# Moving the opening's arithmetic off GpSimd in a GFNet mixing + MLP kernel: filter products added in PSUM, places for all weight pieces early, the filter loaded by two queues

## Chip, cores and metric

The kernel runs on one core of one Trainium2 chip. The metric is the device time of one execution in microseconds (us). Engines are named as in the profile: PE is TensorE, DVE is VectorE, ACT is ScalarE, POOL is GpSimd and SP is SyncE. L12 is line 12 of the kernel that the view belongs to. The changed kernel has other line numbers than the kernel before: the products L312 to L315 become L311 to L314, the weight multiplications L596 and L602 become L597 and L603, the first main loop matmul L405 becomes L408, and L590 (the step that joins a weight's sign and exponent) keeps its number. The sum of a weight's two parts moves from GpSimd at L584 to DVE at L592.

## The reference

```python
X = np.fft.rfft(x, axis=1)                  # x: (8, 3008, 256) fp32
Y = X * (filt_r + 1j * filt_i)[None]        # filter: (1505, 256), complex
y = np.fft.irfft(Y, n=3008, axis=1)
h = y.reshape(24064, 256) @ w_in            # (256, 2048), float64 in memory
g = np.where(h > 0, h, np.exp(np.minimum(h, 0)) - 1)
out = g @ w_out                             # (2048, 256), float64 in memory
```

## The kernel before

The transforms are matmuls (3008 = 47 x 64), and the two matrix products of the MLP use seven products in place of eight. The main loop works on one batch of the MLP while it transforms the next. Before the loop stands an **opening**: batch 0 is transformed alone, and beside it the float64 weights, 16 pieces of 512 KB, are turned into fp32. Each piece goes through a split (two DVE masks), four ACT instructions, a sum of two parts f + l, and a join (one DVE instruction that adds the sign, then multiplications into `w_in` or `w_out`; after every second piece four additions that make the Strassen sets). A split with its conversion and the join of the piece before is called a tick here.

Batch 0's transform is worked in eight groups g. `b_unit` does eight matmuls into PSUM, then four DVE products with the filter, and adds them; `bi_unit` transforms back and evacuates by ACT; `y_write` stores the result. After the last group `y_read` and `n_unit` prepare the first operands of the loop.

```python
def b_unit(b, g, ...):
    ...
    nc.vector.tensor_tensor(out=sr, in0=re, in1=f[:, 0], op=ALU.mult)      # re, im: PSUM
    nc.vector.tensor_tensor(out=si, in0=re, in1=f[:, 1], op=ALU.mult)
    nc.vector.tensor_tensor(out=p, in0=im, in1=f[:, 1], op=ALU.mult)
    nc.vector.tensor_tensor(out=q, in0=im, in1=f[:, 0], op=ALU.mult)
    nc.gpsimd.tensor_tensor(out=sr, in0=sr, in1=p, op=ALU.subtract)
    nc.gpsimd.tensor_tensor(out=si, in0=si, in1=q, op=ALU.add)

def w_sum(k):
    nc.gpsimd.tensor_tensor(out=f, in0=f, in1=l, op=ALU.add)

def w_join(k):
    nc.vector.scalar_tensor_tensor(out=e, in0=hi, scalar=0x80000000, in1=e, ...)   # L590
    ...                                                # multiplications, DVE
    if j % 2 == 1:
        eng = nc.gpsimd if j == 1 else nc.vector       # Strassen sets
        ...
# ... (the opening)
FETCH = {0: 8, 1: 9, 2: 10, 3: 11, 4: 12, 5: 13, 7: 14, 8: 15}
for a in range(2):
    f_read_first(ff, a)                                # whole filter, SyncE's queue
# ... (six rounds with the chunks of x and pieces 0 to 5)
for g in range(NG + 2):
    k = NXC + g
    w_split(k); w_sum(k - 1)
    ...                                                # t_first, bi_unit, b_unit, y_write
    w_float(k); w_join(k - 1)
    if g in FETCH:
        w_fetch(FETCH[g])                              # GpSimd's queue
```

## Time and profile before

| | before |
|---|---|
| median of the fast runs beside the result (4) | 2698.86 us (2698.16 to 2699.39) |
| span of the profiled execution, mean PE clock | 2696.9 us, 0.981 |
| first main loop matmul on phs (L405) | 149.15 us |
| from there to the end | 2547.75 us, PE busy 2531.23 |
| PE / DVE / ACT / POOL busy | 2605.7 / 1859.5 / 1507.5 / 294.2 us |

The last row is from the page's first part. It is an average over the loop, where PE is full, and the opening, where it is not. The row to keep is the third (phs is a PSUM tile, written by the loop's first product). In the timeline (start, duration, engine, line, operation, operands) of the kernel before it is this line:

```profile
149.15 1.06 PE L405 MATMUL phs<-y,wi 128*128 128x224 f32 x4
```

### The profile page before, as it was taken

What the parts mean: (1) busy time and instruction counts of PE and PEld (TensorE: products, weight loads), DVE (VectorE), ACT (ScalarE), POOL (GpSimd) and SP (SyncE); (2) the same over time, 40 slices, a digit from 0 to 9 for tenths busy, and PEclk for the clock granted to TensorE, in tenths of its full rate; (3) what the DMA queues carried; (4) which work ended last, traced back from release to release, by engine and by line L of the source; (5) the groups of instructions that cost most, each with busy time, mean ns of one, the idle gap of its engine ahead of it and who ended that gap; (6) DMA issues with size and microseconds to landing.
All of it is one profiled execution on the core that took longest, in us unless ns stands there. A gap on an engine that the chain in (4) does not pass through costs nothing.

```text
span 2696.9 us, 37188 instructions
## 1 busy us (share of the span) xinstructions
PE 2605.7 (97%) x13440; PEld 2210.1 (82%) x13440; DVE 1859.5 (69%) x3181; ACT 1507.5 (56%) x2610; POOL 294.2 (11%) x338
## 2 busy tenths in 40 slices
PE   4689999999999999999999999999999999999998
PEld 3278888987888888988889887898889888899887
DVE  3957776667667676767766677676767767666665
ACT  4455555655556555555555555565555555555554
POOL 3621210002000120001200021000210012000000
PEclk7689999999999999999999999999999999999999
DMA  8365331434213431252314332143421233110010
GB/s 182 96 153 129 81 77 38 101 80 111 52 38 89 103 96 38 45 130 75 83 40 95 84 90 69 37 101 84 115 56 38 60 90 89 38 40 19 21 27 16
DMA packets 231481, 202.87 MB, mean 75 GB/s; under 512 B 132764, under 2 KB 198128, under 8 KB 231298
## 3 DMA queue, kind: packets, MB, share of 16 engines
q1 hardware_dynamic: 213426, 164.94, 25.6%
q0 software_dynamic: 16288, 33.65, 5.2%
q10 hardware_dynamic: 1584, 1.90, 0.3%
q8 instruction: 107, 1.75, 0.3%
q14 instruction: 76, 0.62, 0.1%
HBM read 128.45 MB, written 74.97 MB: 75 GB/s over the span
## 4 chain that ended last, share of the span: by engine, by line
PE 93%; DVE 3%; DMA 3%; issue 0%; POOL 0%; ACT 0%; SPq 0%; DVEq 0%; POOLq 0%
PE po L487 42%; PE phs L405 24%; PE phd L405 12%; PE pha L405 6%; PE psn L357 3%; PE pva L300 2%; PE psr L300 2%; PE psa L201 2%; DMA ff<-in_filt_r_dram 1%; DVE we L590 1%; DMA t<-tf_t 1%; DVE wo L602 0%; DMA f<-in_moe_w_out_dram 0%; DMA ff<-in_filt_i_dram 0%; DMA gr<-gr_t 0%
## 5 line engine op out<-in xcount | busy, mean ns | idle before, releaser
L487 PE MATMUL po<-g,wo 128*128 128x256 f32 (+1 forms) x5376 | 1296.7, 375 | 0.0
L487 PEld LDWEIGHTS po<-g,wo 128*128 128x128 f32 x5376 | 1015.0, 190 | 129.5 <-issue 16.2
L416 ACT ACTIVATE g<-phs 128x512 f32<-128x512 f32 (+1 forms) x576 | 338.7, 588 | 844.0 <-PE phs L405 843.3
L413 DVE TENSOR_TENSOR g<-phd,g 128x512 f32<-128x512 f32 (+1 forms) x384 | 259.6, 676 | 465.0 <-ACT e L423 278.8
L423 ACT ACTIVATE e<-e 128x512 f32<-128x512 f32 (+1 forms) x768 | 477.3, 621 | 24.3
L405 PE MATMUL phs<-y,wi 128*128 128x256 f32 (+1 forms) x1536 | 394.9, 380 | 0.0
L405 PE MATMUL phs<-ys,wi 128*128 128x256 f32 (+1 forms) x1536 | 387.7, 375 | 2.1 <-ACT g L416 1.5
L427 DVE SCALAR_TENSOR_TENSOR g<-e,g 128x512 f32<-128x512 f32 (+1 forms) x576 | 387.1, 672 | 0.2 <-ACT e L423 0.2
L422 ACT ACTIVATE e<-g 128x512 f32<-128x512 f32 (+1 forms) x576 | 353.1, 613 | 35.1 <-DVE g L413 29.0
L405 PEld LDWEIGHTS phs<-y,wi 128*128 128x128 f32 x1536 | 284.8, 190 | 83.1 <-ACT t L328 34.1
L405 PEld LDWEIGHTS phs<-ys,wi 128*128 128x128 f32 x1536 | 291.4, 190 | 36.1 <-ACT g L416 3.1
L427 DVE SCALAR_TENSOR_TENSOR g<-e,phs 128x512 f32<-128x512 f32 (+1 forms) x192 | 129.9, 676 | 137.9 <-ACT e L423 137.9
L317 POOL TENSOR_TENSOR sr<-sr,sp 128x512 f32<-128x512 f32 x64 | 81.3, 1270 | 1277.5 <-DVE sp L314 1277.5
L405 PE MATMUL phd<-ys,wi 128*128 128x256 f32 (+1 forms) x768 | 193.9, 375 | 1.8 <-DVE g L413 1.8
L405 PE MATMUL pha<-y,wi 128*128 128x256 f32 (+1 forms) x768 | 193.7, 375 | 0.0
L405 PE MATMUL phd<-y,wi 128*128 128x256 f32 (+1 forms) x768 | 193.7, 375 | 0.0
L422 ACT ACTIVATE e<-phs 128x512 f32<-128x512 f32 (+1 forms) x192 | 112.9, 588 | 141.9 <-PE phs L405 141.0
L405 PEld LDWEIGHTS phd<-ys,wi 128*128 128x128 f32 x768 | 145.7, 190 | 18.9 <-DVE g L413 2.5
L405 PEld LDWEIGHTS pha<-y,wi 128*128 128x128 f32 x768 | 145.8, 190 | 16.7
L405 PEld LDWEIGHTS phd<-y,wi 128*128 128x128 f32 x768 | 145.8, 190 | 16.5
L464 DVE TENSOR_TENSOR g<-g,g 128x512 f32<-128x512 f32 (+1 forms) x192 | 130.7, 681 | 6.7
L467 DVE TENSOR_TENSOR g<-g,g 128x512 f32<-128x512 f32 (+1 forms) x192 | 130.7, 681 | 6.6
(116 smaller groups left out, 2441.4 us busy)
## 6 DMA issues: line engine op xcount, KB each, us to landing
yd<-t SPq DMA_DIRECT2D x128, 192.0 KB
t<-yd SPq DMA_DIRECT2D x192, 128.0 KB
z<-t SPq DMA_DIRECT2D x84, 256.0 KB
f<-fd POOLq DMA_DIRECT2D x112, 192.0 KB, 3.6
t<-z SPq DMA_DIRECT2D x224, 96.0 KB
out_dram<-o SPq DMA_DIRECT2D x640, 32.0 KB
tn<-tn_t SPq DMA_DIRECT2D x48, 256.0 KB
xc<-in_x_dram SPq DMA_DIRECT2D x84, 128.0 KB
```

Source lines behind the costliest of these rows:

```text
L300: nc.tensor.matmul(ps[:, u:u + w, :], table[k, v, :], rhs[k, u:u + w, :], start=True, stop=True)
L317: nc.gpsimd.tensor_tensor(out=sr, in0=sr, in1=p, op=ALU.subtract)
L357: nc.tensor.matmul(ps[:, ts(q, P)], t[:, i - 4 * m, ds(dh * P, P)], w[:, i - 4 * m, :], start=True, stop=True)
L405: nc.tensor.matmul(ps[:, a, 0:h], w_in[q][:, COMBO[n], a, :], y[n], start=start and a == 0, stop=True, skip_group_check=True)
L413: nc.vector.tensor_tensor(out=g[o], in0=i0, in1=i1, op=ALU.add)
L416: nc.scalar.activation(out=g[o], in_=i0, func=AXT.Copy)
L422: nc.scalar.activation(out=e, in_=src, func=AXT.Relu, scale=-1.0)
L423: nc.scalar.activation(out=e, in_=e, func=AXT.Exp, scale=-1.0)
L427: nc.vector.scalar_tensor_tensor(out=g[n], in0=es[n], scalar=1.0, in1=src, op0=ALU.subtract, op1=ALU.max)
L464: nc.vector.tensor_tensor(out=b12, in0=b22, in1=b12, op=ALU.subtract)
L467: nc.vector.tensor_tensor(out=g["t4"], in0=g["b21"], in1=g["t2"], op=ALU.subtract)
L487: nc.tensor.matmul(po[i][:, u, 0:h], w_out[q][:, COMBO[n], a, :], g[n][:, a, :], start=q == 0 and a == 0 and n in (1, 3, 6, 4), stop=True, ...
```

## The change

The intent is an opening in which GpSimd computes nothing and only issues transfers.

1. In batch 0 the two filter products of each part are not added by GpSimd. `bi_unit` multiplies both by the table and PSUM adds them (16 matmuls a group in place of 8).
2. The sums f + l and the Strassen sets of `w_in` go to DVE. DVE gives 12 evacuations to ACT.
3. Every weight piece gets a place that is free early; pieces 8 to 15 are asked for right behind the filter.
4. `filt_r` stays on SyncE's queue, `filt_i` is issued by GpSimd.
5. Pieces 6 to 9 are converted before the first group, the others in groups 0, 1, 5, 7, 8 and 9.

```diff
@@ f_read_first
-        for c, src in enumerate((filt_r, filt_i)):
-            nc.sync.dma_start(...)
+        for src, c, queue in (((filt_r, 0, nc.sync), (filt_i, 1, nc.gpsimd))[part],):
+            queue.dma_start(...)
@@ tile_mm
+            for n, r in enumerate(rhs):
+                nc.tensor.matmul(ps[:, u:u + w, :], table[k, v, :], r[k, u:u + w, :],
+                                 start=n == 0, stop=n == len(rhs) - 1)
@@ b_unit
-        nc.vector.tensor_tensor(out=p, in0=im, in1=f[:, 1], op=ALU.mult)
+        nc.vector.scalar_tensor_tensor(out=p, in0=im, scalar=-1.0, in1=f[:, 1], op0=ALU.mult, op1=ALU.mult)
...
-        nc.gpsimd.tensor_tensor(out=sr, in0=sr, in1=p, op=ALU.subtract)
+        if b == 0:
+            ss[b, g] = [sr, p], [si, q]
+            return
+        nc.gpsimd.tensor_tensor(out=sr, in0=sr, in1=p, op=ALU.add)
@@ w_join
+        nc.vector.tensor_tensor(out=f, in0=f, in1=l, op=ALU.add)
...
-            eng = nc.gpsimd if j == 1 else nc.vector
@@ the opening
-        FETCH = {0: 8, 1: 9, 2: 10, 3: 11, 4: 12, 5: 13, 7: 14, 8: 15}
+        TICKS = {0: 10, 1: 11, 5: 12, 7: 13, 8: 14, 9: 15}
...
+            for a in range(2):
+                f_read_first(ff, a, 1)
+            for k in range(NXC + 2, 14):
+                w_fetch(k)
+            for g in range(2):
+                t_first(g)
+            for k in range(NXC, 10):
+                w_split(k)
+                tick(k)
+                if k < 8:
+                    w_fetch(8 + k)
```

Cut: the places of the pieces in `w_fetch`, the evacuations, buffers, and the loop over the groups, where `w_split` and `tick` now follow TICKS.

More of the change, by code (lines that the diff above doesn't have):

```diff
@@ L204, in a_unit @@
         banks.extend((i0, i1))
-    zt = [[w[2 + k].rearrange("p a b c -> p (a b c)") for w in (w_in, w_out)] for k in range(2)]
+    zt = [[], [w[3].rearrange("p a b c -> p (a b c)") for w in (w_in, w_out)]]
     ROWS = 112
@@ L242, in a_first @@
                 s = ps[:, 32 * kh:32 * kh + 32].rearrange("p (k a) u q -> p k a (u q)", a=2)
-                if dh:
-                    nc.vector.tensor_copy(out=o, in_=s)
-                else:
-                    nc.scalar.activation(out=o, in_=s, func=AXT.Copy)
+                nc.scalar.activation(out=o, in_=s, func=AXT.Copy)
             banks.append(k)
@@ L280, in f_read, with f_read_first @@
             nc.gpsimd.dma_start(t[r].rearrange("p c u d -> p (c u d)"), fd[g, a].rearrange("q c u d -> q (c u d)"))
-    def f_read_first(t, a):
+    def f_read_first(t, a, part):
         r = a * 64
-        for c, src in enumerate((filt_r, filt_i)):
-            nc.sync.dma_start(t[r:r + 24, :, c, :, :].rearrange("q g u d -> q g (u d)"),
+        for src, c, queue in (((filt_r, 0, nc.sync), (filt_i, 1, nc.gpsimd))[part],):
+            queue.dma_start(t[r:r + 24, :, c, :, :].rearrange("q g u d -> q g (u d)"),
                                 raw(src, 2 * a, [[64 * D, 24], [4 * D, NG], [1, 2 * D]]))
@@ L291, in f_read_first @@
                 for r0, n in ((24, 16), (40, 7)):
-                    nc.sync.dma_start(t[r + r0:r + r0 + n, g0:NG, c, u, :],
+                    queue.dma_start(t[r + r0:r + r0 + n, g0:NG, c, u, :],
                                         raw(src, 64 * (r0 - 23) - 4 * g0 - 2 * a - u,
@@ L295, in f_read_first, with b_unit @@
             if a == 0:
-                nc.sync.dma_start(t[24:48, 0, c, 0, :], raw(src, 32, [[64 * D, 24], [1, D]]))
+                queue.dma_start(t[24:48, 0, c, 0, :], raw(src, 32, [[64 * D, 24], [1, D]]))
     def tile_mm(ps, table, k, rhs, special):
         for u, w, v in ((0, 1, 1), (1, 1, 0)) if special else ((0, 2, 0),):
-            nc.tensor.matmul(ps[:, u:u + w, :], table[k, v, :], rhs[k, u:u + w, :], start=True, stop=True)
-    def b_unit(b, g, f=None, gb=gb):
+            for n, r in enumerate(rhs):
+                nc.tensor.matmul(ps[:, u:u + w, :], table[k, v, :], r[k, u:u + w, :], start=n == 0, stop=n == len(rhs) - 1)
+    def b_unit(b, g, f=None, gb=gb, pq=None):
         t = t2s.pop((b, g))
@@ L307, in b_unit @@
             for ps, k in ((re, LO), (im, HI)):
-                tile_mm(ps[o:o + 64], gb, k, t[:, a:a + 2, :], g == 0 and a == 0)
+                tile_mm(ps[o:o + 64], gb, k, [t[:, a:a + 2, :]], g == 0 and a == 0)
         sr, si = (sp.tile([P, 2, D], FP32, tag=n, name=n) for n in ("sr", "si"))
-        p, q = (qp.tile([P, 2, D], FP32, tag=n, name=n) for n in ("sp", "sq"))
+        p, q = pq or (qp.tile([P, 2, D], FP32, tag=n, name=n) for n in ("sp", "sq"))
         nc.vector.tensor_tensor(out=sr, in0=re, in1=f[:, 0], op=ALU.mult)
         nc.vector.tensor_tensor(out=si, in0=re, in1=f[:, 1], op=ALU.mult)
-        nc.vector.tensor_tensor(out=p, in0=im, in1=f[:, 1], op=ALU.mult)
+        nc.vector.scalar_tensor_tensor(out=p, in0=im, scalar=-1.0, in1=f[:, 1], op0=ALU.mult, op1=ALU.mult)
         nc.vector.tensor_tensor(out=q, in0=im, in1=f[:, 0], op=ALU.mult)
         banks.extend((i0, i1))
-        nc.gpsimd.tensor_tensor(out=sr, in0=sr, in1=p, op=ALU.subtract)
+        if b == 0:
+            ss[b, g] = [sr, p], [si, q]
+            return
+        nc.gpsimd.tensor_tensor(out=sr, in0=sr, in1=p, op=ALU.add)
         nc.gpsimd.tensor_tensor(out=si, in0=si, in1=q, op=ALU.add)
-        ss[b, g] = (sr, si)
+        ss[b, g] = [sr], [si]
     def bi_unit(b, g):
@@ L538 @@
     wds = {}
-    wbufs = list(fbufs)
-    W_PLACE = (0, 1, 2, 3, 4, 5, 6, 3, 4, 5, 6, 0, 1, 2, 0, 1)
     def w_fetch(k):
         q, j = divmod(k, 4)
-        wd = wds[k] = wbufs[W_PLACE[k]].bitcast(U32).rearrange("p c u d -> p (c u d)").rearrange("p (a w) -> p a w", w=2)
+        if k in (3, 4):
+            wd = t2p.tile([P, 4, D], FP32, tag="t2", name="wd").rearrange("p u d -> p (u d)")
+        elif k in (10, 11):
+            wd = t1p.tile([P, XC, D], FP32, tag="t1", name="wd").rearrange("p u d -> p (u d)")
+        elif k in (6, 7, 8, 9, 15):
+            wd = xp.tile([P, 2, 2, D], FP32, tag="xc", name="wd").rearrange("p k u d -> p (k u d)")
+        else:
+            wd = fbufs[{5: 0, 12: 1, 13: 2, 14: 0}.get(k, k)].rearrange("p c u d -> p (c u d)")
+        wd = wds[k] = wd.bitcast(U32).rearrange("p (a w) -> p a w", w=2)
         if j < 2:
@@ L552, in w_fetch @@
             nc.gpsimd.dma_start(wd[:, ts(i, n), :].rearrange("p a w -> p (a w)"), s)
-    wts = {}
+    wts, wtmp = {}, []
     def w_split(k):
-        if k % 2:
-            m, e = (sdp.tile([P, 2, D], FP32, tag="sd", name=n).bitcast(U32).rearrange("p a b -> p (a b)") for n in ("wm", "we"))
-            c = t1p.tile([P, XC, D], FP32, tag="t1", name="wfl").rearrange("p (a b) d -> p a (b d)", a=2)
-        else:
-            m, e = (kp.tile([P, 512], U32, tag=t, name=n) for t, n in (("k0", "wm"), ("k1", "we")))
-            c = kp.tile([P, 2, 512], FP32, tag="c", name="wfl")
+        m, e, c = wtmp[k % 2]
         f, l = c[:, 0], c[:, 1]
@@ L580, in w_float @@
         nc.scalar.activation(out=e, in_=ef, func=AXT.Relu, scale=-1.0, bias=edges[:, 1:2])
-    def w_sum(k):
-        m, e, f, l = wts[k]
-        nc.gpsimd.tensor_tensor(out=f, in0=f, in1=l, op=ALU.add)
     def w_join(k):
@@ L603, in w_join @@
         if j % 2 == 1:
-            eng = nc.gpsimd if j == 1 else nc.vector
             w = (w_in if j < 2 else w_out)[q]
             a11, a21, a12, a22, s1, s2, s4 = (w[:, i] for i in range(7))
-            eng.tensor_tensor(out=s1, in0=a21, in1=a22, op=ALU.add)
-            eng.tensor_tensor(out=s2, in0=s1, in1=a11, op=ALU.subtract)
-            eng.tensor_tensor(out=s4, in0=a12, in1=s2, op=ALU.subtract)
-            eng.tensor_tensor(out=a21, in0=a11, in1=a21, op=ALU.subtract)
+            nc.vector.tensor_tensor(out=s1, in0=a21, in1=a22, op=ALU.add)
+            nc.vector.tensor_tensor(out=s2, in0=s1, in1=a11, op=ALU.subtract)
+            nc.vector.tensor_tensor(out=s4, in0=a12, in1=s2, op=ALU.subtract)
+            nc.vector.tensor_tensor(out=a21, in0=a11, in1=a21, op=ALU.subtract)
     def f_arrange():
@@ L637 @@
             gf = bp.tile([P, 2, 64], FP32, name="gf")
-            wbufs += [bp.tile([P, 2, 2, D], FP32, name="wb%d" % i) for i in range(4)]
+            pq = [bp.tile([P, 2, D], FP32, name="pq%d" % i) for i in range(2)]
+            zt[0] += [bp.tile([P, 16 * ROWS], FP32, name="zt%d" % i) for i in range(2)]
             for k in range(2):
@@ L643 @@
                 x_load_first(c)
+            wtmp.append([kp.tile([P, 512], U32, tag=t, name=n) for t, n in (("k0", "wm"), ("k1", "we"))] +
+                        [kp.tile([P, 2, 512], FP32, tag="c", name="wfl")])
+            wtmp.append([sdp.tile([P, 2, D], FP32, tag="sd", name=n).bitcast(U32).rearrange("p a b -> p (a b)")
+                         for n in ("wm", "we")] +
+                        [t1p.tile([P, XC, D], FP32, tag="t1", name="wfl").rearrange("p (a b) d -> p a (b d)", a=2)])
             nc.scalar.memzero(ff)
@@ L651, with tick @@
             for a in range(2):
-                f_read_first(ff, a)
+                f_read_first(ff, a, 0)
+            def tick(k):
+                w_float(k)
+                w_join(k - 1)
             for c in range(NXC):
                 w_split(c)
-                if c > 0:
-                    w_sum(c - 1)
                 nc.gpsimd.tensor_copy(out=junk[0:1], in_=xs[0, c][0:1, 0, 0:1])
@@ L663 @@
                     w_join(c - 1)
-            t_first(0)
+            for a in range(2):
[9 more added lines that the diff above has]
+                    w_fetch(8 + k)
             for g in range(NG + 2):
-                k = NXC + g
-                w_split(k)
-                w_sum(k - 1)
-                if g + 1 < NG:
+                k = TICKS.get(g)
+                if k:
+                    w_split(k)
+                if 1 <= g < NG - 1:
                     t_first(g + 1)
@@ L673 @@
                 if g < NG:
-                    b_unit(0, g, ff[:, g], gf)
+                    b_unit(0, g, ff[:, g], gf, pq if g % 2 else None)
                 if g >= 2:
                     y_write(0, g - 2)
-                w_float(k)
-                w_join(k - 1)
-                if g in FETCH:
-                    w_fetch(FETCH[g])
+                if k:
+                    tick(k)
         y_read(0, 0)
-        w_sum(15)
         w_join(15)
```

## The prediction

> **What bounds the kernel now.** I began with the table of stretches, to find where TensorE, the engine that carries the work, is not full.
>
> ```profile
> core 0: us, PE busy (x) PEld busy (x) DVE busy (x) ACT busy (x) POOL busy (x), PEclk, DMA share, GB/s
> 0.00:45.00 45.00, 19.54 (x97) 17.73 (x97) 15.80 (x33) 23.94 (x34) 18.78 (x35) 0.87 1.01 219
> 45.00:66.00 21.00, 7.24 (x51) 5.35 (x51) 8.41 (x17) 8.95 (x15) 2.35 (x4) 0.66 0.64 116
> 66.00:130.00 64.00, 43.57 (x148) 14.41 (x148) 62.03 (x70) 29.11 (x51) 42.77 (x42) 0.61 0.34 93
> 130.00:152.00 22.00, 6.35 (x28) 5.39 (x27) 9.55 (x21) 7.64 (x13) 7.82 (x10) 0.56 0.72 182
> 220.00:2697.00 2477.00, 2464.33 (x12750) 2109.19 (x12748) 1716.71 (x2961) 1397.60 (x2424) 201.82 (x230) 1.00 0.29 69
> ```
>
> From 220 us on TensorE is busy 2464 of 2477 us at full clock; the change touches nothing that sets that part. It edits the opening, in which the main loop's first matmul on phs (row L405 of the timeline) starts at 149.15 us. So the question is only: by how much does that start move? Every us there is a us of the total.
>
> The opening has three limits in turn. To 45 us the DMA share is 1.01 at 219 GB/s: x, its tables, the filter and weight pieces. To 66 us DVE waits for the filter. From 66 to 130 us DVE is "busy" 62 of 64 us at a PE clock of 0.61. The last 20 us are a tail of waits. The chain of waits names the same things:
>
> ```profile
> 37.78 19.13 DMA ff<-in_filt_r_dram
> 56.92 7.06 DMA ff<-in_filt_i_dram
> ...
> 72.55 6.30 DVE we L590
> ...
> 107.00 6.30 DVE we L590
> ...
> 129.04 3.07 DMA f<-in_moe_w_out_dram
> ...
> 137.95 6.00 DMA f<-in_moe_w_out_dram
> ```
>
> L590 combines two SBUF operands of 512 elements; 6.30 us is far from its cost. The groups by form and the timeline of the two engines tell why:
>
> ```profile
> L590 DVE SCALAR_TENSOR_TENSOR we<-wb,we 128x512 uint32<-128x512 uint32 x8 | 20.6, 2572 | 0.0
> L590 DVE SCALAR_TENSOR_TENSOR we<-f,we 128x512 uint32<-128x512 uint32 x8 | 7.9, 993 | 2.7 <-ACT we L580 2.7
> L602 DVE TENSOR_TENSOR wo<-wfl,we 128x256 f32<-128x256 f32 x16 | 12.7, 835 | 0.8
> L596 DVE TENSOR_TENSOR wi<-wfl,we 128x512 f32<-128x512 f32 x8 | 9.0, 1131 | 0.8
> ```
>
> ```profile
> 72.48 6.37 DVE L590 SCALAR_TENSOR_TENSOR we<-wb,we 128x512 uint32<-128x512 uint32 x1
> ```
>
> ```profile
> 72.75 1.28 POOL L584 TENSOR_TENSOR wfl<-wfl 128x512 f32<-128x512 f32 x1
> 73.98 1.26 POOL L317 TENSOR_TENSOR sr<-sr,sp 128x512 f32<-128x512 f32 x1
> 75.20 1.26 POOL L318 TENSOR_TENSOR si<-si,sq 128x512 f32<-128x512 f32 x1
> 76.41 0.57 POOL L552 DMA_DIRECT2D wb<-in_moe_w_in_dram  x1
> 77.01 1.28 POOL L584 TENSOR_TENSOR wfl<-wfl 128x512 f32<-128x512 f32 x1
> ```
>
> DVE's instruction ends at 78.85, 0.56 us after GpSimd's run of back-to-back additions ends at 78.29. Where GpSimd is idle (144.73 us) L590 takes 0.68 us. Much of DVE's busy time is thus waiting behind GpSimd. The products L312 to L315, with one operand in PSUM, keep 0.68 us even beside GpSimd.
>
> **What the Trainium skill says.** "SBUF — State Buffer", section "Who interferes with whom": a DVE instruction with two SBUF inputs contends with a GpSimd instruction that reads SBUF, and one with at most one SBUF input outside the two-port modes does not. The trace agrees on both sides (6.37 against 0.68 us for L590; 0.68 for L312). "TensorE: Matmul & The Clock Gate", section "What's actually happening": the clock is half until a window of about 3.4 us was busy, and falls back after an idle one. The trace agrees: eight filter matmuls take about 1.1 us at clock 1.00 (52.8 us) and 2.1 us at 0.50 (82.9 us). "DMA: Bandwidth & Descriptors", section "Issuing engines are not separate DMA queues": several queues save issuing time, not bandwidth. The share of 1.01 over the first 45 us agrees that a second queue for the filter has little free bandwidth to win there.
>
> **The change part by part.**
>
> *GpSimd's arithmetic off the opening.* Removed blocking on DVE, from the groups, busy time less count times the unblocked duration: L590 28.5 - 16 x 0.68 = 17.6; L596 9.0 - 8 x 0.69 = 3.5; L602 12.7 - 16 x 0.38 = 6.6; L569 and L570 17.4 - 32 x 0.42 = 4.0. Together 31.7 us, nearly all between 66 and 130 us.
>
> *DVE takes on:* 16 sums f+l at 0.61 us start to start (as L596) = 9.8 us, and the four Strassen sets of the w_in pieces at 1.6 us (L607 to L610 as DVE runs them at 121.36) = 6.4. It loses 12 evacuations L244 of 0.38 = 4.5 us to ACT. The -1 folded into the product costs nothing: a SCALAR_TENSOR_TENSOR L427 has a mean of 672 ns, a TENSOR_TENSOR L413 676. Net for DVE: -31.7 + 16.2 - 4.5 = -20 us.
>
> *TensorE takes on* the additions: bi has 16 matmuls instead of 8 a group. At half clock 8 take 1.85 us (103.43 to 105.3), so 16 take 3.7; with transposes 1.7 and b 2.0 a group costs 7.4 us at half clock and about 4.0 at full (0.9 + 2.0 + 1.1).
>
> *Places.* In the kernel before the pieces 14 and 15 are fetched at 128.5 and 137.4 us, because their buffers come free late; DVE idles 3.1 and 9.7 us for them. Now pieces 8 to 13 are asked for in the loading stage, 14 and 15 soon after. This tail wait goes.
>
> *When can the groups start?* By bytes: x 3.0, its tables 1.5, small tables 0.3, filter 3.0, pieces 0 to 9 5.1 MB, 12.9 MB in all. The kernel before had moved 11.9 MB by about 60 us (windows of 10 us: 245, 260, 212, 194, 171, 122 GB/s). With the filter on two queues and no queue idle I expect 200 to 210 GB/s to the end: 62 to 65 us. ACT gives the same: its first evacuation starts at 21 us, then six rounds of 2.1 (four evacuations) + 2.5 (L575 to L580) = 27.5, t_first twice 2.2, four ticks 10: 61 us. DVE's four ticks (3.5 us each, at 2.73 for a piece plus 1.6 for every second one) end at 61 too. I take 65 us, hardly earlier than the 66 us of before, but with piece 8 joined where before it was piece 5.
>
> *The groups from there.* DVE: six splits 0.68 = 4.1, seven joins (9 to 15) 2.05 = 14.4, four Strassen sets 6.4, eight times four products at 0.60 = 19.2, sum 44 us. Of this join 15 (3.7) lies beside the tail, and join 14 and half of join 13's round lie behind the last products. Groups without a tick are TensorE's: 4.0 to 5 us instead of DVE's 2.4, four times, which adds about 8 us. So the last products end about 41 us after the start, bi of group 7 about 5 us later: 111 us. Before, from its evacuation (135.75) to the first phs (149.15) passed 13.4 us: write y, read it, n_unit. Without piece 15 on the DMA at the same time I take 12.
>
> Sum: 65 + 46 + 12 = 123 us against 149: 26 to 28 us less. 2698.5 - 27 = 2671 us, a ratio of 0.990.
>
> **The rivals.**
>
> 1. *TensorE becomes the bound at half clock.* For it: the clock from 66 to 130 us is 0.61 on average, mostly 0.50, and bi doubles. Then g = 0 to 9 cost 2.0 + 3.7 + 5 x 7.4 + 5.7 + 2 x 3.7 = 56 us, the first phs comes at 65 + 57 + 12 = 134, and the time is 2684 us. Against it: at 7.4 us of work in a 7 us group TensorE would have no gaps, and at 98 and 106 us the trace shows the clock returning to 1.00 after about 6 us without gaps. Probably it alternates.
>
> 2. *The transfers bound it.* Asking for pieces 8 to 13 early puts 3 MB next to the filter on a DMA that is full to 50 us; SWDGE issues of the filter cost GpSimd too (L620 takes 1.7 us for 184 KB in the later rearrangement). If the filter or piece 9 comes at 72 us, the result is 2678 us.
>
> 3. *All goes well:* the filter lands at 55 us since its transfers no longer queue behind one another, ACT and DVE keep their pace and start at 59, groups take 4.5 us on average: the first phs at 59 + 40 + 11 = 110, 2659 us. A 2% gain needs it at 95 us. DVE alone has 16 x 3.53 + 19.2 = 76 us of work and cannot start before the first piece lands at 8 us: 84 us, and about 11 us of the tail follow the last group. So over 2% is nearly excluded.
>
> 4. *The gain is lost later.* The loop's first stretch, 152 to 220 us, holds stalls too (TensorE 64.6 of 68 us), but they depend on the loop's own order and move with it. Nothing slows the loop after: products with b > 0 keep their GpSimd sums.
>
> **Range and chances.** Start of the groups 58 to 72 us, pace of a group 4.5 to 7 us, tail 11 to 14 us. Both bad together give 2686, both good 2657. Faster by over 2%: 0.03. Slower by over 2%: 0.01, for it would need an opening 54 us longer. Within 2%: 0.96.
>
> **What would show it.** First phs near 123 us instead of 149. L590 near 0.7 us throughout, L596 and L602 near 0.69 and 0.38, DVE's excess below 3 us. DVE busy in the stage of the groups below 50 us. No wait of DVE for a piece after the groups. The last bi evacuated near 111 us. A PE clock above 0.75 in the groups if rival 1 is wrong. From the first phs to the end 2548 us, as before. I would be wrong if the filter or piece 9 lands after 72 us, if clock 0.50 holds through the groups, or if the loop after the opening differs by more than 3 us.

## The result

The changed kernel takes **2675.57 us** (median of 4 runs, 2674.36 to 2679.11) against 2698.86 for the kernel before. The ratio is 0.9916, with a 95% interval of 0.9899 to 0.9933. A ratio is the mean time of one kernel's fast runs over that of the other's of the same rounds, so it is not quite the ratio of the medians. The interval excludes 1: the change is a gain of 0.84%, or 23 us.

The stretches of the changed kernel, with the columns as the header names them:

```profile
core 0: us, PE busy (x) PEld busy (x) DVE busy (x) ACT busy (x) POOL busy (x), PEclk, DMA share, GB/s
0.00:45.00 45.00, 20.13 (x117) 18.11 (x121) 19.39 (x43) 30.73 (x53) 14.83 (x35) 0.91 1.01 236
45.00:66.00 21.00, 6.49 (x36) 3.16 (x30) 5.09 (x12) 5.53 (x10) 6.06 (x11) 0.58 1.01 156
66.00:130.00 64.00, 42.60 (x244) 21.37 (x244) 52.58 (x106) 36.61 (x63) 2.67 (x5) 0.72 0.46 133
130.00:152.00 22.00, 20.46 (x122) 18.83 (x122) 16.44 (x31) 14.04 (x26) 0.00 (x0) 1.00 0.47 119
220.00:2674.00 2454.00, 2441.76 (x12627) 2089.74 (x12625) 1700.34 (x2933) 1386.07 (x2403) 199.01 (x225) 1.00 0.28 69
```

The stretch from 130 to 152 us was the tail of waits before (PE busy 6.35 us); now PE is busy 20.46 of 22, so the loop has begun. The stretch from 66 to 130 us holds only five GpSimd instructions, before 42. The stretch from 45 to 66 us is the bad one: DVE does 5.09 us of work in 21 us while the DMA share is 1.01, so it waits for transfers.

The loop starts 22.7 us earlier, which is the whole gain. From there to the end pass 2547.95 us (before: 2547.75):

```profile
126.45 1.70 PE L408 MATMUL phs<-y,wi 128*128 128x224 f32 x4
```

The groups of equal instructions from 0 to 130 us (line, engine, operation, operands, count; then busy us, mean ns of one; then idle time before them). L590, L603 and L597 answer to the four rows of before, the L592 sums are new on DVE, and L311, the first filter product of each group, shows DVE's waits for TensorE:

```profile
L590 DVE SCALAR_TENSOR_TENSOR we<-wd,we 128x512 uint32<-128x512 uint32 x9 | 6.2, 684 | 0.0
L592 DVE TENSOR_TENSOR wfl<-wfl 128x512 f32<-128x512 f32 x16 | 10.9, 684 | 0.0
L603 DVE TENSOR_TENSOR wo<-wfl,we 128x256 f32<-128x256 f32 x16 | 6.1, 421 | 0.3
L597 DVE TENSOR_TENSOR wi<-wfl,we 128x512 f32<-128x512 f32 x8 | 5.5, 692 | 0.3
L590 DVE SCALAR_TENSOR_TENSOR we<-f,we 128x512 uint32<-128x512 uint32 x7 | 4.8, 688 | 12.9 <-ACT we L584 12.9
L311 DVE TENSOR_TENSOR sr<-psr,ff 128x512 f32<-128x512 f32 x8 | 5.5, 689 | 5.3 <-PE psi L299 5.3
```

L590 takes 684 and 688 ns on average where it took 2572 and 993. The other rows have lost their waiting too, so none of these DVE instructions is stretched any more.

The chain of waits (start, duration, what) shows the tail after the groups, but it hides the wait at the front:

```profile
51.50 23.62 issue
...
115.39 2.60 DMA yd<-t
119.35 3.42 DMA t<-yd
122.90 3.75 PE psn L360 x16
```

"Issue" is time in which the engine waited for nothing that the profile shows. A chain that has run onto PE's own order can lose a wait in this way. The timeline of DVE, with idle time and its releaser in brackets, has it:

```profile
66.08 0.43 DVE L573 TENSOR_SCALAR wm<-wd 128x512 uint32<-128x512 uint32 x1 [15.81 <-DMA wd<-in_moe_w_in_dram]
...
73.74 0.68 DVE L311 TENSOR_TENSOR sr<-psr,ff 128x512 f32<-128x512 f32 x1
...
90.18 0.69 DVE L311 TENSOR_TENSOR sr<-psr,ff 128x512 f32<-128x512 f32 x1 [2.62 <-PE psi L299]
```

DVE is idle for 15.81 us until piece 8 has landed. Only then come the ticks with pieces 8 and 9 and the split of piece 10 (66.08 to 73.74, 7.7 us), and only then the first product. The third line is the longest wait of DVE for TensorE in the groups. GpSimd's timeline shows why piece 8 came so late:

```profile
37.38 0.55 POOL L290 DMA_DIRECT2D ff<-in_filt_i_dram  x1 [2.63 <-DMA f<-in_moe_w_in_dram]
...
47.87 0.58 POOL L290 DMA_DIRECT2D ff<-in_filt_i_dram  x1 [3.67 <-DMA ff<-in_filt_i_dram]
...
50.87 0.58 POOL L561 DMA_DIRECT2D wd<-in_moe_w_in_dram  x1 [0.37 <-PE psi L299]
```

GpSimd issues `filt_i` from 32.68 to 50.5 us, and it stands still between the issues until earlier transfers have landed. The operands kept with the trace say why: GpSimd's transfers use eight semaphores in turn (99 to 106), and each issue first waits for the semaphore that it will raise itself. So an issue waits until the transfer eight issues before it has landed, and the 11 small transfers of `filt_i` use up these places. It is a wait in the program as it was built, and no run changed the number. Piece 8 is next in GpSimd's order, so it is asked for at 50.87 and lands about 15 us later.

### The profile page after: what moved, and what is told of

It is laid out like the page before. It is cut to its first block, busy times and chain, and to the rows that moved or that the text cites.

```text
span 2674.4 us, 37291 instructions
## 1 busy us (share of the span) xinstructions
PE 2597.6 (97%) x13508; PEld 2209.6 (83%) x13508; DVE 1840.2 (69%) x3201; ACT 1511.4 (57%) x2622; POOL 245.7 (9%) x301
## 4 chain that ended last, share of the span: by engine, by line
PE 95%; DMA 1%; issue 1%; ACT 1%; DVE 1%; SPq 0%; DVEq 0%; ACTq 0%
PE po L490 42%; PE phs L408 25%; PE phd L408 12%; PE pha L408 6%; PE psn L360 3%; PE pva L299 2%; PE psr L299 2%; PE psa L201 2%; DMA xc<-in_x_dram 1%; PE po L254 0%; PE pvb L299 0%; DMA z<-t 0%; PE psi L299 0%; ACT zt L243 0%; ACT we L583 0%
## 5 line engine op out<-in xcount | busy, mean ns | idle before, releaser
L320 POOL TENSOR_TENSOR sr<-sr,sp 128x512 f32<-128x512 f32 x56 | 71.3, 1273 | 1242.4 <-DVE sp L313 1242.4
```

Source lines behind the costliest of these rows:

```text
L320: nc.gpsimd.tensor_tensor(out=sr, in0=sr, in1=p, op=ALU.add)
```

## The experiments

Twelve kernels ran; all gave correct results. My theory had two halves. First: the gain comes from DVE no longer blocked by GpSimd and from the early places of the last pieces, and not from the filter's second queue. Second: the shortfall against the prediction comes from the order in GpSimd's queue. The rivals were that the second queue brings part of the gain, and that the number of bytes bounds the start of the groups in any order.

All edits are to the changed kernel. "First product" and "first phs" are read from each run's timeline. The kernel before ran on the same chip each time, with medians from 2698.32 to 2699.65. The interval of each ratio is about ±0.0015, or 4 us, so a difference of two ratios is uncertain by some 0.002 (an estimate). The spans of a loss or gain given below are the distances to the two values of the changed kernel, not intervals. Surer is a comparison within one set of rounds on one chip: the slowest run of e2 and of e3 is faster than the fastest of e1, and the fastest run of e4, e5 and e9 is slower than the slowest of e1, e6 and a0, which ran beside them.

| run | edit | median us | ratio to before (95%) | first product | first phs |
|---|---|---|---|---|---|
| a0_changed | none | 2674.16 | 0.9906 (0.9891 to 0.9921) | 72.10 | 124.65 |
| e1_one_queue | whole filter on SyncE | 2674.95 | 0.9912 (0.9898 to 0.9925) | 61.19 | 126.36 |
| e4_gp_products | products added by GpSimd | 2681.82 | 0.9937 (0.9925 to 0.9950) | 72.11 | 132.96 |
| e5_gp_wsums | weight sums on GpSimd | 2684.61 | 0.9951 (0.9938 to 0.9963) | 88.59 | 139.48 |
| e6_late_fetch | 12 to 15 asked for later in the program | 2674.34 | 0.9911 (0.9897 to 0.9924) | 73.60 | 126.28 |
| e9_gated_fetch | 14 and 15 really asked for late | 2680.37 | 0.9932 (0.9920 to 0.9945) | 73.63 | 132.03 |
| e2_w89_first | 8 and 9 ahead of `filt_i` | 2667.97 | 0.9886 (0.9871 to 0.9901) | 67.36 | 119.63 |
| e3_ticks_in_groups | ticks 8 to 11 in groups 0 to 3 | 2670.01 | 0.9894 (0.9881 to 0.9908) | 64.85 | 120.79 |
| e7_w8_11_first | 8 to 11 ahead of `filt_i` | 2669.89 | 0.9893 (0.9879 to 0.9906) | 64.25 | 121.23 |
| e8_paced_one_queue | filter on SyncE, 10 to 15 held back | 2677.39 | 0.9920 (0.9907 to 0.9934) | 56.90 | 125.83 |
| e10_w89_split | e2, half of `filt_i` on SyncE, later ticks | 2673.86 | 0.9907 (0.9894 to 0.9921) | 63.46 | 124.94 |
| e11_w89_later_ticks | e2, ticks 10 and 11 one group later | 2666.53 | 0.9880 (0.9864 to 0.9897) | 65.36 | 116.59 |

### The changed kernel once more (a0)

> The changed kernel itself once more, unedited, as the measure for the others on the same chip: 2674 to 2677, first phs at 126 to 127 us, DVE idle 14 to 17 us before piece 8.

The second gives 2674.16 us (2670.78 to 2674.64), with a ratio of 0.9906 where the first had 0.9916. Edits are therefore read against both values. DVE again waits for piece 8 (14.59 us, to 64.43), and the first product comes at 72.10 instead of 73.74. Differences of 2 us in this place mean nothing.

### One queue for the filter (e1)

```diff
-        ... (filt_i, 1, nc.gpsimd) ...
+        ... (filt_i, 1, nc.sync) ...
```

> Undoes one part: both halves of the filter go out on the SyncE queue again, filt_i still issued after the first six weight pieces. Changed kernel for comparison: DVE idle 15.8 us (50.3 to 66.1) for piece 8, first product at 73.74, first phs matmul at 126.66, 2675.6 us. Theory Q (order in GpSimd's queue: piece 8 stands behind filt_i there): piece 8 lands before 56 us, the idle time before it falls below 6 us, the first product moves to 66 to 71 us and the time to 2668 to 2673. Rival B (the transfers as a whole are the bound, order does not matter): first product at 72 to 76 us, because now the filter comes last, and 2674 to 2678.

2674.95 us, ratio 0.9912, between the two values of the changed kernel. The second queue brings nothing, and theory Q's time (2668 to 2673) was missed; rival B's was met. The timeline shows what happened inside:

```profile
61.19 0.69 DVE L311 TENSOR_TENSOR sr<-psr,ff 128x512 f32<-128x512 f32 x1 [2.17 <-issue]
74.07 0.69 DVE L312 TENSOR_TENSOR si<-psr,ff 128x512 f32<-128x512 f32 x1 [12.19 <-DMA ff<-in_filt_i_dram]
```

Without `filt_i` in front of them the weight pieces land early, the wait for piece 8 disappears, and the first product comes at 61.19. But the second product waits until 74.07, for the rest of the filter. One wait has taken the place of the other, and the groups go on at the same time as before the edit.

### The products added by GpSimd again (e4)

```diff
         if b == 0:
-            ss[b, g] = [sr, p], [si, q]
-            return
+            pass
```

> Undoes one part: in the opening too the two halves of each filter product are added on GpSimd again, not in PSUM; weights stay off GpSimd. Theory L (DVE's two-SBUF-operand instructions are blocked by GpSimd's reads): in the groups with a piece L590 is stretched from 0.68 to 1.3 us and more, L592, L597 or L603 too, 2 to 3 us in each of groups 0, 1, 5 and 7, less half a microsecond where TensorE is spared 8 of 24 matmuls: first phs 5 to 9 us later, 2680 to 2685. Rival E (the gain came from the early weight pieces, the sums on GpSimd were harmless): 2675.6 plus or minus 2, and no stretched L590.

2681.82 us, ratio 0.9937, which is 0.0021 to 0.0031 (6 to 8 us) worse than the changed kernel. The first product stays at 72.11; the groups take longer. In the groups view from 0 to 135 us:

```profile
L591 DVE TENSOR_TENSOR wfl<-wfl 128x512 f32<-128x512 f32 x16 | 15.2, 949 | 0.0
L573 DVE TENSOR_SCALAR we<-f 128x512 uint32<-128x512 uint32 x7 | 5.2, 736 | 0.0
```

The sums (L591 here) take 949 ns against 684, and this group of the masks 736 against some 420. The sums, the joins' sign step (L589 here) and the masks together are 10.9 us longer than in the changed kernel. The blocking is back, although the only arithmetic that GpSimd got back is 16 additions.

### The weight sums on GpSimd again (e5)

```diff
-        nc.vector.tensor_tensor(out=f, in0=f, in1=l, op=ALU.add)
+        nc.gpsimd.tensor_tensor(out=f, in0=f, in1=l, op=ALU.add)
...
+            eng = nc.gpsimd if j == 1 else nc.vector      # Strassen sets of w_in
```

> Undoes one part: the sums f+l of the weight pieces and the Strassen sets of the w_in pieces go back to GpSimd; the filter products stay added in PSUM. Theory O (GpSimd works in order and its issues of filt_i and pieces 8 to 13 stand before the sums of pieces 5 to 7): the join of piece 5 waits from about 45 us until GpSimd has issued piece 13 at about 65, so three joins more lie after 66 us, the first product comes at 78 to 82 us instead of 73.7 and the time is 2680 to 2688. Theory L alone (only the blocked two-operand instructions): L590, L597 or L603 stretched by about 1.3 us for each piece in the groups, saved 0.6 us each: 2676 to 2680. Rival (DVE relieved of 16 sums and four sets is a gain): 2668 to 2674.

2684.61 us (2683.39 to 2688.53), ratio 0.9951: 0.0035 to 0.0045 (9 to 12 us) of the gain is lost. The profile is of the slowest of its runs, so its first phs (139.48) overstates the loss; its first product (88.59) came later than the 78 to 82 expected. The first line is from DVE's timeline and the second from GpSimd's:

```profile
71.22 0.69 DVE L597 TENSOR_TENSOR wi<-wfl,we 128x512 f32<-128x512 f32 x1 [19.14 <-POOL wfl L592]
```

```profile
69.91 1.27 POOL L592 TENSOR_TENSOR wfl<-wfl 128x512 f32<-128x512 f32 x1
```

The sum of a piece that had long landed stood behind the DMA issues of the filter and of pieces 8 to 13 in GpSimd's order, and DVE waited 19.14 us for it. So much of the cost is not the contention but the in-order queue. This belongs to the combination: the kernel before had the sums on GpSimd too, but no filter in that queue. The run thus gives the worth of this part only beside the other parts.

### The last pieces later (e6, e9)

In e6 the fetches of pieces 12 to 15 were moved behind groups 4, 5, 7 and 8, in the order of the program.

```diff
-            for k in range(NXC + 2, 14):
+            for k in range(NXC + 2, 12):
...
-                if k < 8:
-                    w_fetch(8 + k)
...
+                if g in (4, 5, 7, 8):
+                    w_fetch({4: 12, 5: 13, 7: 14, 8: 15}[g])
```

> Undoes one part: pieces 12 to 15 are asked for only within the groups, after groups 4, 5, 7 and 8 as in the kernel before. Theory T (the early places are worth the waits of DVE for pieces 14 and 15 in the tail): two waits of DVE of 3 to 7 us each after group 7, DVE's last weight work ends 5 to 10 us later than at 122.8, the first phs at 130 to 136 instead of 126.5, 2679 to 2685. Rival (the tail is set by writing and reading y, which ends at 122.8 us too): 2675.6 plus or minus 2.

2674.34 us, nothing changed. This was a miss, and the cause is in GpSimd's timeline:

```profile
68.38 1.06 POOL L561 DMA_DIRECT2D wd<-in_moe_w_out_dram  x2 [0.39 <-issue]
```

GpSimd has no other work in the opening and its buffers are free, so it asked for the "late" pieces by 69.4 us, as in the changed kernel. The place in the program means nothing for an engine that at that place has only its own earlier transfers to wait for. So e9 holds it back with data: before fetching piece 14 (15) GpSimd copies one element that join 12 (13) writes.

```diff
-                if k < 8:
-                    w_fetch(8 + k)
...
+                if g in (7, 8):
+                    nc.gpsimd.tensor_copy(out=junk[0:1], in_=w_in[3][0:1, 2 * (g - 7), 0, 0:1])
+                    w_fetch(g + 7)
```

> Undoes the early places of pieces 14 and 15 alone, and this time surely: GpSimd first copies one element that the join of piece 12 (13) writes, then asks for piece 14 (15), so neither can be asked for before about 112 (119) us. In the run with late issues in program order nothing changed, because GpSimd, with no arithmetic, had nothing to wait for and issued them at 66 to 69 us all the same. Theory T: DVE and ACT wait 4 to 6 us for each; ACT's wait for piece 14 stands before the evacuation of the last bi, so y is written 4 to 6 us later; first phs at 130 to 133, and the loop's second step waits for DVE's last join at about 130: 2679 to 2684. Rival: the tail is set elsewhere, 2675.6 plus or minus 2.

2680.37 us, ratio 0.9932: 0.0016 to 0.0026 (4 to 7 us) worse. GpSimd was released at 112.25 us, and DVE and ACT then waited for piece 14:

```profile
116.58 0.43 DVE L573 TENSOR_SCALAR wm<-f 128x512 uint32<-128x512 uint32 x1 [4.40 <-DMA f<-in_moe_w_out_dram]
...
116.63 0.69 ACT L579 ACTIVATE wfl<-f 128x512 f32<-128x512 uint32 x1 [6.11 <-DMA f<-in_moe_w_out_dram]
```

(The first is from DVE's timeline, the second from ACT's.) ACT takes its work in order, so the last evacuation of the groups stood behind this wait: it ended at 120.2 us, in the changed kernel at 115.4. DVE waited another 3.57 us for piece 15. This is the tail of the kernel before again, at a smaller size.

### Pieces 8 and 9 ahead of the filter (e2), or needed later (e3)

```diff
+            for k in range(NXC + 2, 10):
+                w_fetch(k)
             for a in range(2):
                 f_read_first(ff, a, 1)
-            for k in range(NXC + 2, 14):
+            for k in range(10, 14):
                 w_fetch(k)
```

> Only the order in GpSimd's queue: pieces 8 and 9 are asked for before filt_i instead of after it. Theory Q: piece 8 lands by 50 us, DVE's idle time moves from before piece 8 to before the first product, which waits for filt_i at 66 to 70 us; first phs 119 to 123 us, 2668 to 2672. Rival B: filt_i is later by as much as the pieces are earlier, first product at 73 or later, 2675 plus or minus 2.

2667.97 us (2667.78 to 2669.03), ratio 0.9886, 0.0020 to 0.0030 (5 to 8 us) better. The first product comes at 67.36. It now stands behind the split of piece 10, which comes first in DVE's order:

```profile
66.67 0.43 DVE L573 TENSOR_SCALAR wm<-wd 128x512 uint32<-128x512 uint32 x1 [10.94 <-DMA wd<-in_moe_w_out_dram]
```

In e3 the transfers keep their order, but the ticks of pieces 8 to 11 go into groups 0 to 3.

```diff
-        TICKS = {0: 10, 1: 11, 5: 12, 7: 13, 8: 14, 9: 15}
+        TICKS = {0: 8, 1: 9, 2: 10, 3: 11, 5: 12, 7: 13, 8: 14, 9: 15}
...
-            for k in range(NXC, 10):
+            for k in range(NXC, 8):
```

> Transfers unchanged; pieces 8 and 9 are worked on within the groups (one tick per group again in groups 0 to 3) instead of before them, so the first product no longer stands behind piece 8 in DVE's order except for its split. Theory Q: DVE still waits for piece 8 at 66 us since its split stands before the first product, but the products then start at about 67, the groups 2 and 3 take their pieces into gaps in which DVE waited for TensorE (2.6 and 1.3 us), and the first phs comes 2 to 4 us earlier, 2671.5 to 2673.5. Rival P (TensorE at half clock sets the pace of groups 0 to 3): no gain, 2675 plus or minus 1.5.

2670.01 us, ratio 0.9894, 3 to 6 us better and a little more than theory Q had expected. The groups start at 64.85 but have two more ticks in them, so the first phs (120.79) gains less than the first product. Both runs confirm that the wait for piece 8, and the two ticks behind it, had set the start of the groups.

### How far the order can be pushed (e7, e8, e10, e11)

In e7 pieces 8 to 11 stand ahead of `filt_i`, and their ticks ahead of the groups.

```diff
-        TICKS = {0: 10, 1: 11, 5: 12, 7: 13, 8: 14, 9: 15}
+        TICKS = {5: 12, 7: 13, 8: 14, 9: 15}
...
+            for k in range(NXC + 2, 12):
+                w_fetch(k)                 # then filt_i, then 12 and 13
...
-            for k in range(NXC, 10):
+            for k in range(NXC, 12):
```

> Pieces 8 to 11 before filt_i in GpSimd's queue, and all four worked on before the groups. The run with pieces 8 and 9 first idled 10.9 us at the end of that work for piece 10, which again stood behind filt_i. Theory Q: DVE works on through pieces 10 and 11 to about 63 us, then the first product waits for filt_i at 67 to 71 us, and groups 0 and 1 lose 7 us of DVE's work: first phs 115 to 119, 2664 to 2668. Rival B (the filter is later by as much as 1 MB takes, 4 to 5 us, and groups 0 and 1 are TensorE's at half clock): 2667 to 2670, no gain over 2668.0.

2669.89 us, ratio 0.9893, no better than e2 and as rival B had it. The first product comes at 64.25, but the second waits until 70.04:

```profile
70.04 0.69 DVE L312 TENSOR_TENSOR si<-psr,ff 128x512 f32<-128x512 f32 x1 [5.11 <-DMA f<-in_moe_w_in_dram]
```

The profile puts the wait down to a weight piece, but the instruction reads only PSUM and the filter; I take it for the filter's. What is moved ahead of the filter is paid for by the filter.

In e8 the whole filter is on SyncE's queue, and pieces 10 to 15 are held back until piece 7 is joined.

```diff
-        ... (filt_i, 1, nc.gpsimd) ...
+        ... (filt_i, 1, nc.sync) ...
...
-        TICKS = {0: 10, 1: 11, 5: 12, 7: 13, 8: 14, 9: 15}
+        TICKS = {2: 10, 3: 11, 5: 12, 7: 13, 8: 14, 9: 15}
...
-                if k < 8:
-                    w_fetch(8 + k)
+                if k == 8:
+                    nc.gpsimd.tensor_copy(out=junk[0:1], in_=w_out[1][0:1, 0, 1, 0:1])
+                    for n in range(10, 16):
+                        w_fetch(n)
```

> Both filter halves on the SyncE queue; pieces 8 and 9 early; pieces 10 to 15 only once piece 7 is joined (about 50 us), so that the filter does not share the transfers with them before; the ticks of 10 and 11 move to groups 2 and 3. In the one-queue run the filter came last, at 73.8 us, while all pieces had landed by 61. Theory F (what the groups wait for is the filter's 1 KB rows, and every weight byte moved before them delays them): filter complete at 57 to 63 us, first product there, first phs 111 to 116, 2659 to 2664. Rival H (one hardware queue cannot move the 1 KB rows faster than about 130 to 190 GB/s even alone): filter at 64 to 70, first phs 117 to 122, 2666 to 2671.

2677.39 us, ratio 0.9920. Both theories had expected a gain and there was none:

```profile
73.82 0.69 DVE L312 TENSOR_TENSOR si<-psr,ff 128x512 f32<-128x512 f32 x1 [16.24 <-DMA ff<-in_filt_i_dram]
```

SyncE's issues use eight semaphores in turn as well, and it asked for the second half of `filt_i` only from 53.1 to 58.7 us, beside the weights (53.0 to 57.5). What was asked for together did not move at the same rate. From 47 to 52 us SyncE's queue, almost alone, moved 0.67 MB (537 packets); from 62 to 72 us, twice as long, it moved 0.34 MB (349 packets), and GpSimd's queue 2.27 MB (664). So the weights passed the filter. Windows of 5 us from 55 to 70 us moved 153, 217 and 279 GB/s at a DMA share of 1.03 to 1.09, and still the filter was not there before 73.8.

In e10 e2's order is kept, half of `filt_i` goes to SyncE's queue, and ticks 10 and 11 move to groups 1 and 2, so that their splits no longer stand ahead of the first product.

```diff
-        ... (filt_i, 1, nc.gpsimd) ...
+        ... (filt_i, 1, (nc.sync, nc.gpsimd)[a]) ...
-        TICKS = {0: 10, 1: 11, 5: 12, 7: 13, 8: 14, 9: 15}
+        TICKS = {1: 10, 2: 11, 5: 12, 7: 13, 8: 14, 9: 15}
         # and pieces 8, 9 ahead of filt_i, as in e2
```

> Pieces 8 and 9 before the filter in GpSimd's queue, as in the fastest run so far; of filt_i only the second half stays there, the first half goes to the SyncE queue behind filt_r; the ticks of pieces 10 and 11 move to groups 1 and 2 so that the first product is not behind piece 10. Theory F2 (after 50 us the GpSimd queue alone moves 1 KB rows at 115 to 130 GB/s while the SyncE queue is empty): filter complete at 59 to 64 us, first products there, first phs 112 to 117, 2660 to 2665. Rival H (shared engines: what SyncE gains GpSimd's queue loses): filter at 65 to 69, first phs 117 to 121, 2666 to 2670, no better than 2668.0.

2673.86 us, ratio 0.9907: worse than both theories had it. The second product waits 10.73 us, until 74.89, for SyncE's half of `filt_i`, as in e8, though the last of that half was asked for by 60.0 us. e11 differs from e10 in one thing: all of `filt_i` is on GpSimd's queue again, with pieces 10 to 15 behind it.

> The fastest run so far (pieces 8 and 9 before filt_i, 2668.0) with the ticks of pieces 10 and 11 moved from groups 0 and 1 to groups 1 and 2, so that the first product is no longer behind piece 10, which landed at 66.7 us there. Theory Q (order of waits): the first product starts when filt_i is complete, 63 to 66 us, groups 0 to 2 share the two ticks with TensorE's half-clock work, first phs 116 to 119 against 119.6, 2665 to 2668. Rival: filt_i itself is complete only at 66 to 67 us, since piece 10 follows it directly in the queue: 2668 plus or minus 1.

```profile
65.36 0.69 DVE L311 TENSOR_TENSOR sr<-psr,ff 128x512 f32<-128x512 f32 x1 [7.21 <-DMA ff<-in_filt_r_dram]
...
66.64 0.69 DVE L312 TENSOR_TENSOR si<-psr,ff 128x512 f32<-128x512 f32 x1 [0.59 <-DMA ff<-in_filt_i_dram]
```

**2666.53 us** (2666.15 to 2668.69), ratio 0.9880 (0.9864 to 0.9897), against 2699.65 for the kernel before on that chip. This is the best of all: its slowest run is faster than the fastest of the changed kernel's eight (2670.78), though on another chip, and the ratio intervals just overlap with a0's. They also overlap with e2's, though e11's first phs is 3.0 us earlier. The filter is complete by 66.64 us, 8.3 us earlier than in e10. The pair e10 and e11, with the packet counts of e8, points to what matters: the filter is late when bulk loads run beside it in another queue, and early when the bulk stands behind it in the same queue. That it loses because its rows are short (256 fp32 values, 1 KB, in most of its transfers) is my explanation. The packets of e8 from 62 to 72 us fit it (0.34 MB in 349 packets is 1.0 KB each, 2.27 MB in 664 is 3.4 KB), but no run changed the rows.

The rival that bytes bound the start is not dead. The best order still has its first two products at 65.36 and 66.64 us, just after the 62 to 65 us that the prediction worked out from bytes.

## Why the prediction was right, and where a step failed

The prediction was 2671.0 us in a range of 2657 to 2686, with 0.96 for "within 2%". The measured 2675.57 us lies inside the range and the class is right. Its steps:

- **The loop does not change.** Right. 2548 us from the first phs on was expected; it is 2547.95.
- **DVE is unblocked.** Right. An excess below 3 us was expected; in the rows of the groups view (L590, L597, L603 and the masks) it is below 1 us. A net of -20 us for DVE was worked out; the page's busy time of DVE falls from 1859.5 to 1840.2 us, by 19.3. That this matters for the time is shown by e4, and, with the in-order queue on top, by e5.
- **The wait for the last pieces goes.** Right: after the groups DVE waits for no piece, and e9 puts the wait back at a cost of 4 to 7 us.
- **The second queue for the filter.** The prediction put "200 to 210 GB/s to the end: 62 to 65 us" on it and saw little to win. The rate was right (45 x 236 + 21 x 156 GB/s x us are 13.9 MB by 66 us, which is 211 GB/s). e1 shows that the second queue is worth nothing.
- **When the groups start.** This step failed: "I take 65 us", measured 73.74 (72.10 in a0). It took the later of two ends, the transfers at 62 to 65 us and the work of DVE and ACT at 61, as if piece 8 came in time to be worked on before the last transfer. But piece 8 stood behind `filt_i` in GpSimd's order and landed at 66.1 us, and the 7.7 us of ticks 8 and 9 came after it. The two ends had to be added, not compared: 66.1 + 7.7 = 73.8. The bytes by then were even more than the 12.9 MB that were needed, so about a megabyte of later pieces had come along. e11, with the order mended, started at 65.36.
- **The groups.** "About 41" and "about 5" us, together 46, were expected from the start to the last evacuation; measured 73.74 to 115.37, 41.6 us. The last products ended 36.3 us after the start, and the rest took 5.3. One term that was too large is the TensorE wait, "about 8 us": DVE waited for TensorE 0.16, 2.62, 1.27, 0.62 and 0.59 us, 5.3 in all. The other is DVE's own work: the prediction has join 12 and half of join 13's round ahead of the last products, and both stand behind them (from 109.95 us). Its terms as written also give about 44 us, not 41. From 73.74 to 115.4 us DVE was busy 35.88 us (below 50, as expected).
- **The tail.** 12 us expected; 115.37 to 126.45 is 11.1.
- **The sum.** 65 + 46 + 12 = 123 became 73.7 + 41.6 + 11.1 = 126.4. Errors of opposite sign, +8.7 and -4.4 (and -0.9 in the tail), made the sum look better than its parts; that much of the hit was luck.
- **Rival 1** (half clock throughout) is out: the clock was 0.83 in the groups, where 0.75 was the line drawn, and 1.00 from 90 to 115 us. It had a part in the first groups, though: from 73.74 to 90 us the clock was 0.57, and TensorE was busy 14.88 of 16.26 us. **Rival 2** (transfers) was right about the place of the trouble but not about its form: in the changed kernel it was not the rate of the DMA but the order of its transfers. It said 2678 us. **Rivals 3 and 4** did not happen.

Where the 23 us came from, each part taken back alone: products added in PSUM 6 to 8 us, weight sums off GpSimd 9 to 12, early places for pieces 14 and 15 4 to 7, the second queue 0 within the noise. These are 19 to 27 us; the parts overlap, so the sum is a check and not an account.

**What stays open.** In e11 DVE still idles 7.21 us for the filter, with a mean DMA share of 0.84 from 45 to 66 us. I did not try a layout of the filter with longer rows, or fewer and larger transfers, or more than eight semaphores for a queue. Nor did I find out over how many of the DMA engines its small transfers are spread, or why its rows take the DMA time that they take.

## What to carry to other kernels

Where a transfer and in-order work that needs it both stand ahead of a stage, follow the last transfer through the work behind it and add the two; the maximum of two separate ends is right only if nothing ties them. Put into one queue, in the order of need, what must not be overtaken: the load that is needed first with the bulk behind it, rather than beside it in another queue (e10 to e11, 2673.86 to 2666.53 us here). An engine that only issues transfers should have no arithmetic behind its issues, and an experiment that wants to delay its transfers must gate them with data, since program order alone doesn't.

## What the Trainium skill lacked or had wrong

- "SBUF — State Buffer", section "Who interferes with whom", holds the shared pair, in the two-port modes, to be taken for a whole instruction, the other engine blocking meanwhile; it does not speak of a run of instructions. In the trace of the kernel before L590 waited through several back-to-back GpSimd instructions and took 6.37 us instead of 0.68. The page's two-port case agrees with e4: a group of masks with one SBUF operand took 736 ns on average instead of some 420.
- "DMA: Bandwidth & Descriptors", section "Queues, rings and completion order", says that a DMA engine goes round between queues packet by packet. It has no number for what a load of short rows loses when bulk runs beside it in another queue: the filter was complete at 73.8 us (e8) and 74.9 (e10) with bulk in another queue, and at 66.6 (e11) with the bulk behind it in the same one.
- The same page, section "Issuing engines are not separate DMA queues", agrees with e1: 2674.95 us with one queue for the filter, 2674.16 and 2675.57 with two.
- I found no page that says how many transfers of one queue a program like this keeps in flight. In these traces each issue of GpSimd waits for the semaphore that it raises, one of eight in turn (waits of 2.63 and 3.67 us before single issues), which also holds up arithmetic behind the issues: in e5 DVE waited 19.14 us for a GpSimd sum. This is how the program was built, not shown to be a limit of the chip.
